# A new order for the 1,035 steps of a sparse-attention and SwiGLU kernel on one core

## The chip, the cores and the metric

The kernel runs on one core of one Trainium2 chip. The metric is the device time of one execution in microseconds (us). The time before is the median of three runs, 237.2 us (235.59, 237.2 and 237.91). A profile of one execution gives the start and the duration of each instruction on each engine: TensorE (PE), its weight loads (PEld), VectorE (DVE), ScalarE (ACT), GpSimd (POOL) and SyncE (SP), which here does nothing but start transfers.

## The reference

Two things are computed, one after the other. First, attention with four batches, eight heads, 768 positions and head size 64, in which each query sees the first 8 keys ("global") and the last 96 before it ("local"), with a bias that falls linearly with distance:

```python
scores = q @ k.T / sqrt(64)
keep   = (key < 8) | ((query - key >= 0) & (query - key < 96))
dist   = where(global and not local, 96, abs(query - key))
scores = where(keep, scores - slope[head] * dist, -1e9)   # slope = 2 ** -(head + 1)
a      = softmax(scores)
attn   = a @ v                                             # 4 x 8 x 768 x 64
```

Then the heads of each position are laid side by side, and the 3,072 rows of 512 pass a gated feed-forward layer:

```python
x    = attn as (3072, 512)
g    = x @ w_gate            # 512 -> 1536
out  = (g * sigmoid(g) * (x @ w_val)) @ w_out   # 1536 -> 512
```

Inputs and outputs are fp32; the kernel computes with fp16 operands and sums in fp32.

## The kernel before

**One list sets the order.** The kernel is written as some forty small functions, each of which issues one step: one load, one group of matmuls, one exponential, one copy. A string, `ORDER` (from line 67), names 1,035 steps with their arguments, such as `g.2.6` or `Lr.3.0.4`. A table (L757) maps each name to its function, and one loop runs the list from the front to the back:

```python
for step in ORDER.split():
    name, *args = step.split(".")
    WORK[name](*(int(a) if a.isdigit() else a for a in args))
```

Scheduling is manual (`tc.manual_schedule()`), so each engine runs its own instructions in the order in which they stand in this list, and nothing is moved between them. The waits between engines follow from the data: a step waits for what it reads, and for the last user of a buffer that it takes. What is planned here is nothing but the position of each step among those of its engine, and, for steps with a letter at their end, the engine: V is VectorE, A is ScalarE, P is GpSimd, and S is a transfer started by SyncE.

**Attention.** Batch 0 comes in two halves of 384 positions, since TensorE has nothing else to do at the start. Its first two head pairs are loaded as fp32 (`Lf`, started by SP and ScalarE) and cast to fp16 (`cast`); all else is loaded by GpSimd, whose transfers cast on the way: key and query halves (`Lh`), four heads of batch 1 (`L4`, L333), single heads of batches 2 and 3 (`Lr`, L344; the arguments are batch, 0 for keys or 1 for queries, and head), value chunks (`Lv`, L292; batch and one of seven chunks), gate and value weights (`Lw`, L351) and output weights (`Lo`, L356). Keys and queries are turned by TensorE (`T`, `U`) with a copy out of PSUM (`k`, `q`, `kw`, `qw`), or by a transposing transfer that SP starts (`D`, L483) into `kN` or `qT`; `K` (L490 to L493) spreads transposed keys into chunks of 120 behind the 8 global ones.

Scores (`C` early, `c` later, L520) go to PSUM, ScalarE takes exponentials of them into `at` (`E`, `x`, L530), VectorE multiplies by masks (`m`, L539), which ScalarE has made from distances (`M`, L384). TensorE then sums the probabilities (`w`, L597 and L630) and weighs the values (`V` for the first half of batch 0; `W`, L614). VectorE inverts the sums (`i`), `j` copies them beside each other, `r` spreads them, and `p` scales the weighed values into `xT`, the input of the feed-forward layer.

Each batch has a value buffer `vS`. Its unused rows are cleared (`Z`, L307 to L310, two memsets). The eight global rows, which arrive with chunk 0, are copied into the later chunks (`G`, L296 to L305): by a transfer of SP, or by an engine. `X` (L319) copies the values to the other half of the partitions.

**Feed-forward.** The 3,072 tokens are eight tiles of 384. For each tile t and each of twelve blocks f of 128 columns there are a gate product (`g.t.f`) and a value product (`v.t.f`), four matmuls of 128x384 each (L693), then a tanh on ScalarE (`t`), and two operations on VectorE (`s` and `h`), which fill `hT`. Output products (`o`, L734, three matmuls of 512 columns each, four steps for each 128 tokens) and the store (`e`) follow. Tiles 0 and 1 are batch 0, and so on; feed-forward work of one batch stands among the attention of the next.

**Buffers.** PSUM is eight banks. A step takes one or two of those that are free at its place in the list, in a fixed rule, and `release` gives them back; so the list also decides which bank a step gets, and for whose last reader it waits. Buffers in SBUF rotate: a new tile of a tag takes the buffer that has been out longest. The tags `kst` and `qst` (staging of keys and queries) have two buffers, `vS` two, `vX` two, `kN` two, `qT` four, `xT` four, `hT` three. A staging tile comes into being with the first load that asks for its batch:

```python
def stage(b, i):
    if (b, i) not in stages:
        shape = [128, H, J * D] if b == 1 else [128, NP, J, 2, D]
        stages[b, i] = sb2.tile(shape, FP16, name=("kst", "qst")[i], tag=("kst", "qst")[i])
    return stages[b, i]
```

In the order before, the keys' staging is asked for by batch 0 (fp32 and fp16 tiles), then batch 1, 2 and 3, and `vS` by batch 0, 1, 3 and 2 (`Z.3.P` stands ahead of `Z.2.P`).

Of the kernel before, what the change touches and what calls it, by code (L numbers as in the profile page):

```python
# [73 lines left out]
E.2.1 r.0.0.0.0 G.0.1.4.V Lw.0.2.1 E.3.1 r.0.0.0.1 b.2.0 E.3.0 T.0.1.0 C.2.0 q.3.1.V k.0.1.A E.2.0  # L74
T.3.1.0 T.0.1.1 T.2.1.0 T.1.1.0 T.1.1.1 k.1.1.A k.3.1.V q.0.1.A q.1.1.V w.0.0.1 Lw.1.0.0 k.2.1.V
q.2.1.A c.0.0.1.1 i.0.0.1 V.1 V.2 V.0 Lw.0.2.0 r.0.1.0.1 Lv.0.5 B.1.1.1 M.0.1 p.0.0.0.0.V Lv.0.6
p.0.0.0.1.V x.0.0.1.1 c.0.1.1.1 B.1.1.0 r.0.1.0.0 Lv.0.4 x.0.1.1.1 p.0.1.0.0.V V.3 c.0.0.1.0 Ld.P.0
c.0.1.1.0 p.0.1.0.1.V X.0.0.2.4.V Lw.1.2.1 Lw.1.2.0 L4.0.0 M.1.1 Lr.1.0.5 Lr.1.0.7 x.0.0.1.0 g.0.0
g.0.3 g.0.1 g.0.2 x.0.1.1.0 m.0.0.1.1.V L4.1.0 t.0.3 t.0.0 m.0.0.1.0.V Lr.1.0.6 w.0.1 v.0.3 t.0.2
s.0.3 v.0.2 s.0.0 i.0.1 s.0.2 Lr.1.1.6 t.0.1 Lw.0.1.1 v.0.0 h.0.2 j.0.1.A X.0.1.2.4.A Lr.1.0.4 h.0.0  # L80
Lr.1.1.4 Lw.0.1.0 g.0.8 g.0.9 r.0.0.1.1 t.0.8 D.1.3.0 X.0.0.4.7.A s.0.1 s.0.8 r.0.0.1.0 r.0.1.1.0
g.0.10 Lw.1.1.0 Lr.1.1.7 h.0.3 v.0.1 Lr.1.1.5 X.0.1.4.7.A t.0.10 t.0.9 h.0.1 s.0.10 g.0.11 W.0.1.0
W.0.1.1 v.0.8 p.0.0.1.1.V p.0.0.1.0.V v.0.10 v.0.9 D.1.2.0 D.1.3.1 r.0.1.1.1 p.0.1.1.0.V v.0.11
p.0.1.1.1.V g.1.10 v.1.3 s.0.9 t.0.11 t.1.10 g.1.0 s.0.11 h.0.10 g.1.1 U.1.0 h.0.8 h.0.11 h.0.9
Z.3.P s.1.10 U.0.1 U.1.1 U.0.0 t.1.0 s.1.0 t.1.1 g.1.11 kw.1.V kw.0.A v.1.10 v.1.1 qw.0.A Lv.1.6
qw.1.A g.1.2 g.1.8 g.1.3 t.1.11 s.1.1 s.1.11 t.1.8 v.1.0 t.1.3 t.1.2 h.1.10 h.1.1 M.1.0 s.1.3 v.1.2
g.0.6 h.1.0 v.1.11 s.1.8 g.1.9 s.1.2 Lv.1.1 M.0.0 g.1.6 h.1.2 Lw.1.1.1 h.1.3 t.1.9 g.0.5 s.1.9
Lr.2.1.3 h.1.11 c.1.0.0.0 t.0.6 t.0.5 t.1.6 s.0.6 c.1.0.0.1 x.1.0.0.1 D.1.2.1 v.1.8 Lv.1.5 g.1.4
s.1.6 g.0.7 g.0.4 h.1.8 s.0.5 v.1.9 v.0.6 Lr.2.0.4 Lv.1.0 t.0.7 x.1.0.0.0 s.0.7 M.3.0 h.1.9 K.1.3
Lo.0 Lo.1 g.1.7 t.0.4 v.1.6 c.1.0.1.0 h.0.6 t.1.7 s.0.4 s.1.7 v.0.7 Lo.2 Lr.2.0.0 h.1.6 v.1.4 Lv.1.2  # L90
h.0.7 v.1.7 t.1.4 g.1.5 v.0.4 Lv.1.4 s.1.4 v.0.5 Lv.1.3 h.1.7 t.1.5 v.1.5 K.1.2 h.1.4 h.0.4 Lr.2.0.3
h.0.5 c.1.1.1.1 Lr.2.1.2 c.1.1.0.0 x.1.0.1.0 c.1.1.0.1 s.1.5 h.1.5 M.2.1 o.0.1.0 o.0.2.0 x.1.1.1.1
# [717 lines left out]
```

## Time and profile before

| | |
|---|---|
| median of three runs | 237.2 us (235.59 to 237.91) |
| span of the profiled execution | 235.1 us, which is also the only time that the profile gives for it |
| instructions | 6,093 |
| TensorE clock granted | 1.000 of full speed |
| data moved by transfers | 25.97 MB, most of it in GpSimd's queue |
| TensorE busy | 228.1 us, 97% of the span |
| VectorE, ScalarE, GpSimd busy | 166.8, 117.0 and 79.1 us |

The profile's first block gives the busy time of each engine and its share of the span. A row of the chain of waits has a start, a duration, and the line that held the end up at that time. A row of the instruction groups names the engine, line and operation, the tile written and the tile read, and a count; behind it stand the total busy time and the mean of one in ns. A row of the timeline has a start, a duration, an engine and a line; in square brackets stands how long the engine was idle ahead of it, and what ended that. In a row of the waits, the operation that waited stands to the left of the arrow and what it waited for to the right, then the idle time in us, the count, and the longest one. A row of the stretches has start and end, length, and then, for TensorE, its weight loads, VectorE, ScalarE and GpSimd, the busy time and the number of instructions; the last columns are the granted clock, the DMA share and the GB/s.

### The profile page before, as it was taken

What the parts mean: (1) busy time and instruction counts of PE and PEld (TensorE: products, weight loads), DVE (VectorE), ACT (ScalarE), POOL (GpSimd) and SP (SyncE); (2) the same over time, 40 slices, a digit from 0 to 9 for tenths busy, and PEclk for the clock granted to TensorE, in tenths of its full rate; (3) what the DMA queues carried; (4) which work ended last, traced back from release to release, by engine and by line L of the source; (5) the groups of instructions that cost most, each with busy time, mean ns of one, the idle gap of its engine ahead of it and who ended that gap; (6) DMA issues with size and microseconds to landing.
All of it is one profiled execution on the core that took longest, in us unless ns stands there. A gap on an engine that the chain in (4) does not pass through costs nothing.

```text
span 235.1 us, 6093 instructions
## 1 busy us (share of the span) xinstructions
PE 228.1 (97%) x2504; PEld 132.2 (56%) x2504; DVE 166.8 (71%) x385; ACT 117.0 (50%) x220; POOL 79.1 (34%) x113
## 2 busy tenths in 40 slices
PE   7889999998899999999999999999999999999997
PEld 5556556555455656655555565556655565554444
DVE  2698996888549798877798998979776467461020
ACT  4679736783546703827826687744231334140421
POOL 8985778664264079787700000000000000000000
DMA  6999999999999999999999610200000120000323
GB/s 170 190 179 205 203 189 185 130 137 146 202 149 163 204 163 136 110 144 138 146 179 197 68 47 3 89 3 0 3 0 0 45 92 1 0 25 22 134 91 134
DMA packets 88324, 25.97 MB, mean 110 GB/s; under 512 B 78048, under 2 KB 85256, under 8 KB 88296
## 3 DMA queue, kind: packets, MB, share of 16 engines
q0 software_dynamic: 67120, 14.25, 78.7%
q1 hardware_dynamic: 20488, 10.74, 24.5%
q10 hardware_dynamic: 688, 0.59, 0.7%
q8 instruction: 19, 0.31, 0.6%
q14 instruction: 9, 0.07, 0.1%
HBM read 28.93 MB, written 6.29 MB: 150 GB/s over the span
## 4 chain that ended last, share of the span: by engine, by line
PE 65%; DMA 23%; POOL 6%; DVE 3%; issue 1%; ACT 0%; SPq 0%; DVEq 0%; POOLq 0%; ACTq 0%
PE banks L693 39%; PE banks L734 20%; DMA vS<-in_v_dram 6%; DMA kst<-in_k_dram 5%; DMA wv<-in_moe_w_val_dram 4%; DMA qst<-in_q_dram 4%; DMA k<-in_k_dram 3%; PE banks L614 2%; PE banks L520 2%; POOL vS L292 1%; DMA out_dram<-osb 1%; PE banks L723 1%; POOL qst L344 1%; POOL q L284 1%; PE banks L630 1%
## 5 line engine op out<-in xcount | busy, mean ns | idle before, releaser
L699 ACT ACTIVATE th<-banks 128x384 f32<-128x384 f32 x96 | 43.9, 493 | 68.1 <-PE banks L693 66.5
L693 PE MATMUL banks<-xT,wv 128*128 128x384 f16 x384 | 71.7, 326 | 0.4 <-DMA wv<-in_moe_w_val_dram 0.3
L693 PE MATMUL banks<-xT,wg 128*128 128x384 f16 x384 | 70.6, 326 | 0.0
L709 DVE TENSOR_TENSOR hT<-banks,sl 128x384 f16<-128x384 f32 x96 | 50.9, 551 | 22.8 <-PE banks L693 19.8
L734 PE MATMUL banks<-wo,hT 128*128 128x512 f16 x276 | 65.3, 379 | 0.6 <-DMA wo<-in_moe_w_out_dram 0.6
L703 DVE SCALAR_TENSOR_TENSOR sl<-th,banks 128x384 f32<-128x384 f32 x96 | 50.2, 546 | 19.3 <-ACT th L699 18.8
L693 PEld LDWEIGHTS <-wv 128*128 128x128 f16 x384 | 36.8, 98 | 26.3 <-DMA wv<-in_moe_w_val_dram 0.7
L693 PEld LDWEIGHTS <-wg 128*128 128x128 f16 x384 | 37.2, 98 | 25.5 <-DVE xT L678 0.2
L734 PEld LDWEIGHTS <-hT 128*128 128x128 f16 x276 | 26.3, 98 | 29.2 <-DMA wo<-in_moe_w_out_dram 0.8
L530 ACT ACTIVATE at<-banks 128x1008 f16<-128x1008 f32 (+3 forms) x28 | 25.7, 957 | 10.6 <-PE banks L520 9.6
L292 POOL DMA_DIRECT2D vS<-in_v_dram x28 | 25.1, 906 | 5.9 <-DMA qst<-in_q_dram 3.0
L752 ACT ACTIVATE osb<-banks 128x512 f32<-128x512 f32 x23 | 13.5, 597 | 20.0 <-PE banks L734 16.5
L539 DVE TENSOR_TENSOR at<-at,masks 128x1008 f16<-128x1008 f16 (+3 forms) x26 | 16.2, 645 | 5.3 <-ACT at L530 4.9
L344 POOL DMA_DIRECT2D qst<-in_q_dram x20 | 16.8, 843 | 8.4 <-DMA wo<-in_moe_w_out_dram 5.2
L344 POOL DMA_DIRECT2D kst<-in_k_dram x20 | 16.7, 839 | 5.5 <-DMA wo<-in_moe_w_out_dram 2.0
L663 DVE STREAM_TRANSPOSE rb<-dR 128x384 f32<-128x384 f32 x32 | 17.1, 555 | 0.1
L678 DVE TENSOR_TENSOR xT<-banks,rb 128x384 f16<-128x384 f32 x22 | 11.0, 542 | 1.0 <-PE banks L614 0.8
L319 ACT COPY vX<-vS 64x1792 f16<-64x1792 f16 (+2 forms) x7 | 9.0, 1287 | 3.3 <-DMA vS<-in_v_dram 3.1
L520 PEld LDWEIGHTS <-kT 64*64 64x64 f16 x456 | 7.4, 107 | 5.5 <-issue 5.1
L520 PE MATMUL banks<-qT,kT 64*64 64x152 f16 (+9 forms) x456 | 9.1, 214 | 0.9 <-DMA qT<-qst 0.7
L614 PE MATMUL banks<-at,vS 64*64 64x152 f16 (+9 forms) x228 | 8.0, 213 | 0.4 <-DVE hT L709 0.4
L614 PEld LDWEIGHTS <-vS 64*64 64x64 f16 x228 | 6.7, 107 | 2.4 <-issue 2.4
(77 smaller groups left out, 150.6 us busy)
## 6 DMA issues: line engine op xcount, KB each, us to landing
out_dram<-osb SPq DMA_DIRECT2D x23, 256.0 KB, 2.5
vS<-in_v_dram POOLq DMA_DIRECT2D x24, 120.0 KB, 8.4
kst<-in_k_dram POOLq DMA_DIRECT2D x20, 96.0 KB, 7.5
qst<-in_q_dram POOLq DMA_DIRECT2D x20, 96.0 KB, 7.2
wg<-in_moe_w_gate_dram POOLq DMA_DIRECT2D x6, 256.0 KB, 8.1
wv<-in_moe_w_val_dram POOLq DMA_DIRECT2D x6, 256.0 KB, 8.4
wo<-in_moe_w_out_dram POOLq DMA_DIRECT2D x3, 512.0 KB, 13.5
k<-in_k_dram POOLq DMA_DIRECT2D x3, 192.0 KB, 6.0
```

The source lines that it names most:

```text
L292: nc.gpsimd.dma_start(out=v_of(b)[r0:r0 + n, c, heads(g), :], in_=v[b, heads(g), KC * c:KC * c + n, :].rearrange("h p d -> p h d"))
L344: nc.gpsimd.dma_start(out=rows_of(i, b, h // 2)[:, :, h % 2, :], in_=KQ[i][b, h].rearrange("(t p) d -> p t d", p=128))
L520: nc.tensor.matmul(sc[64 * r:64 * r + 64, hi, col:col + n], lhsT=kTs[2 * g + r][d, k0:k0 + 64], rhs=qTs[b, 2 * g + r][d, q0:q0 + n], start ...
L530: nc.scalar.activation(out=at[:, :, 0:w], in_=sc[:, :, 0:w], func=AF.Exp, scale=scale)
L539: ENG[e].tensor_mul(a2, a2, masks[:, 2 * g:2 * g + 2, x:x + w])
L614: nc.tensor.matmul(num[64 * hi:64 * hi + 64, r, q0 - HB * half:q0 - HB * half + n], lhsT=vSs[b][k, c, h] if up == r else crossed[b][k, c, ...
L663: nc.vector.transpose(rb.rearrange("p (n i) -> p n i", i=32), rbs[b, half][:, g, r].unsqueeze(2).broadcast_to([128, TB // 32, 32]))
L693: nc.tensor.matmul(gv[t, f, which][:, 0:TB], lhsT=w[:, c, 128 * f:128 * f + 128], rhs=xTs[t][:, c, :], start=(c == 0), stop=(c == NC - 1))
L699: nc.scalar.activation(out=th, in_=gv[t, f, 0][:, 0:TB], func=AF.Tanh, scale=0.5)
L703: nc.vector.scalar_tensor_tensor(out=sl, in0=gv[t, f, "t"], scalar=1.0, in1=gv[t, f, 0][:, 0:TB], op0=AluOp.add, op1=AluOp.mult)
L709: nc.vector.tensor_mul(hTs[t][:, f, :], gv[t, f, 1][:, 0:TB], gv[t, f, "s"])
L734: nc.tensor.matmul(ops_t[t, i], lhsT=hTs[t][:, f, 128 * i:128 * i + 128], rhs=wo[:, f, :], start=(f == 0), stop=(f == NFF - 1))
```

## The change

The string `ORDER` is replaced by another; no function is touched. It holds the same 1,035 steps. 24 of them have another engine letter, all others differ in their place alone. The changes that matter for the steps of the prediction:

- **Start.** `kz` and one clear (`Z.0.P`) lead GpSimd's work; the second clear (`Z.1`) goes to VectorE, further back. The early table `Ld.S.2` is SP's first load. `fill.10` stands ahead of `fill.5`. Three casts move to ScalarE and one to VectorE; key copies `k.1.0` and query copy `q.3.0` go to VectorE, `k.3.1`, `q.2.0` and `q.3.1` to ScalarE, `q.2.1` to VectorE. Keys and queries of both halves of batch 0 (`Lh`) are loaded ahead of all but one value chunk; then three chunks come in a row (`Lv.0.2 Lv.0.1 Lv.0.3`) and two gate weights in a row (`Lw.0.0.0 Lw.0.0.1`). The global rows `G.0.4.7` go from SP to VectorE.
- **Sums of the second half** (`w.0.1`): the gate products `g.0.0` and `g.0.1` no longer stand ahead of it, and mask `M.1.1` is made earlier, `M.3.1` later.
- **Loads of the middle.** Batch 1's loads are ordered anew. `Lr.3.0.4` now stands ahead of `Lr.2.0.7`: batch 3's keys ask for staging before batch 2's. The three output weights follow `Lr.2.0.7` at once, and six of the seven value chunks of batch 1 follow these.
- **Clears and copies later.** `Z.2` and `Z.3` go from GpSimd to VectorE, and batch 2's clear stands ahead of batch 3's. `G.2.1.7` goes from SP to VectorE. Some of `j` and `X` and three of `kw` and `qw` change between VectorE and ScalarE.
- All feed-forward steps stand in another order too, down to the last output products.

```diff
 ORDER = """
-pre Z.0.P Lf.A.1.1 Lf.S.0.1 fill.5 Z.1.P Lf.A.1.0 kz.P Li cast.0.1.V cast.1.0.V cast.1.1.A fill.10
-sl.1 Lh.0.0.4.8 sl.2 Ld.P.1 sl.0 T.1.0.0 T.1.0.1 Ld.S.2 sl.3 T.0.0.1 k.1.0.A sl.4 q.1.0.A q.0.0.V
-b.1.1 Lf.S.0.0 Lh.1.0.4.8 sl.5 sl.7 cast.0.0.V b.1.0 Lh.1.1.4.8 C.1.1 Lv.0.0 C.1.0 E.1.1 Lh.0.1.0.4
-T.0.0.0 b.2.1 b.0.0 E.1.0 k.0.0.V sl.6 b.0.1 T.2.0.0 T.3.0.0 C.0.1 k.2.0.V k.3.0.V Lh.1.1.0.4
-Lh.0.1.4.8 C.0.0 Lv.0.3 Lv.0.1 T.3.0.1 Lv.0.2 E.0.1 T.2.0.1 E.0.0 q.2.0.V G.0.4.7.S pk b.3.0
-Lw.0.0.0 Lw.0.0.1 q.3.0.A w.0.0.0 b.3.1 i.0.0.0 Lw.1.0.1 T.3.1.1 M.3.1 C.3.0 T.2.1.1 C.2.1 C.3.1
...
-g.0.3 g.0.1 g.0.2 x.0.1.1.0 m.0.0.1.1.V L4.1.0 t.0.3 t.0.0 m.0.0.1.0.V Lr.1.0.6 w.0.1 v.0.3 t.0.2
...
-Z.3.P s.1.10 U.0.1 U.1.1 U.0.0 t.1.0 s.1.0 t.1.1 g.1.11 kw.1.V kw.0.A v.1.10 v.1.1 qw.0.A Lv.1.6
...
-s.1.6 g.0.7 g.0.4 h.1.8 s.0.5 v.1.9 v.0.6 Lr.2.0.4 Lv.1.0 t.0.7 x.1.0.0.0 s.0.7 M.3.0 h.1.9 K.1.3
-Lo.0 Lo.1 g.1.7 t.0.4 v.1.6 c.1.0.1.0 h.0.6 t.1.7 s.0.4 s.1.7 v.0.7 Lo.2 Lr.2.0.0 h.1.6 v.1.4 Lv.1.2
...
-W.1.1.0 h.2.6 W.1.1.1 Z.2.P v.2.3 Lr.3.1.7 s.2.0 p.1.1.1.1.V e.0.1 p.1.1.1.0.V g.2.9 r.1.0.1.1
...
-c.2.1.0.0 c.2.1.0.1 x.2.1.0.1 o.2.2.1 o.2.2.2 t.3.7 G.2.1.7.S K.2.0 Lv.2.5 o.2.2.3 Lr.3.1.1 v.3.11
...
+Ld.S.2 Li Lf.A.1.0 pk pre kz.P Lf.S.0.1 sl.2 Lf.S.0.0 Z.0.P fill.10 Lh.0.0.4.8 Lf.A.1.1 sl.3 sl.7
+sl.0 fill.5 cast.1.0.A Lh.1.0.4.8 cast.1.1.V cast.0.1.A b.1.0 cast.0.0.A sl.6 T.0.0.1 T.1.0.0 sl.1
+sl.5 Ld.P.1 T.1.0.1 b.1.1 q.1.0.A T.0.0.0 Lh.0.1.4.8 q.0.0.V T.2.0.0 k.1.0.V Lv.0.0 b.0.1 k.0.0.V
+C.1.0 C.1.1 T.3.0.1 k.2.0.V q.3.0.V T.3.0.0 E.1.0 C.0.1 Lh.1.1.4.8 E.1.1 sl.4 Lh.0.1.0.4 b.0.0 C.0.0
+T.2.0.1 E.0.1 E.0.0 Lh.1.1.0.4 k.3.0.V Lv.0.2 b.3.0 Lv.0.1 b.3.1 b.2.1 Lv.0.3 w.0.0.0 q.2.0.A
+Lw.0.0.0 Lw.0.0.1 Z.1.V Lw.1.0.1 M.1.1 C.3.1 G.0.1.4.V C.2.1 Lw.1.0.0 E.2.1 i.0.0.0 E.3.1 C.3.0
+G.0.4.7.V T.3.1.1 T.3.1.0 T.2.1.1 b.2.0 Lw.0.2.0 E.3.0 k.3.1.A C.2.0 E.2.0 q.2.1.V T.0.1.0 T.1.1.1
...
+p.0.1.0.1.V g.0.3 g.0.2 x.0.1.1.0 x.0.1.1.1 Lw.1.2.0 t.0.2 m.0.0.1.1.V m.0.0.1.0.V Lw.1.2.1 w.0.1
...
+D.1.3.0 h.1.10 s.1.3 Lr.3.0.4 h.1.2 D.1.3.1 Lr.2.0.7 Lo.0 g.0.6 t.1.8 t.0.6 v.1.9 v.1.8 s.1.8
+D.1.2.1 Lo.1 h.1.3 v.1.1 t.1.9 s.1.9 M.3.0 h.1.8 g.1.5 h.1.1 g.1.6 s.0.6 t.1.5 g.1.7 g.0.4 h.1.9
+t.1.6 Lo.2 s.1.5 c.1.0.0.1 c.1.0.0.0 v.1.6 s.1.6 t.1.7 M.2.1 x.1.0.0.0 g.0.7 Lv.1.4 Lv.1.2 v.1.5
+h.1.6 x.1.0.0.1 v.0.6 Z.2.V s.1.7 g.0.5 K.1.3 v.1.7 K.1.2 g.1.4 v.0.7 t.0.7 Lv.1.5 t.0.5 M.0.0 s.0.7
+Lv.1.6 Lv.1.1 h.1.5 v.1.4 h.0.6 v.0.4 s.0.5 t.1.4 v.0.5 t.0.4 h.1.7 s.1.4 Lv.1.3 s.0.4 Lr.2.0.5
...
+D.2.0.0 g.3.11 Lv.3.0 t.2.5 h.3.1 Lv.3.4 s.2.5 c.2.1.1.1 t.3.2 s.3.2 x.2.1.1.1 D.2.1.1 v.2.8 s.2.10
...
+c.2.0.0.1 s.3.6 c.2.0.0.0 x.2.0.0.0 o.2.1.1 g.3.7 v.3.0 o.1.1.0 m.2.0.1.1.V o.2.1.2 G.2.1.7.V
...
 """
```

More of the change, by code (lines that the diff above doesn't have):

```diff
@@ new lines @@
+W.2.1.1 p.2.0.0.1.V r.2.1.1.1 o.2.0.2 r.2.1.0.1 p.2.1.0.0.V o.2.0.3 n.2.1.1 v.3.3 p.2.1.0.1.V g.4.11
+r.2.1.1.0 g.4.3 g.4.1 h.3.10 e.2.0 K.3.3 g.4.8 D.3.1.0 t.4.11 t.4.3 h.3.3 v.4.11 Lv.3.6 s.4.3 s.4.11
+h.4.11 v.4.1 t.4.8 s.4.8 t.4.1 g.4.6 K.3.0 v.4.8 s.4.1 t.4.6 c.3.1.1.1 x.3.1.1.1 p.2.1.1.1.V
+c.3.1.0.0 x.3.1.0.0 s.4.6 g.4.10 p.2.1.1.0.V h.4.8 o.3.1.0 o.3.1.1 K.3.1 c.3.1.0.1 h.4.1 r.2.0.1.0
+t.4.10 Lv.3.1 Lr.3.1.2 c.3.1.1.0 D.3.1.1 x.3.1.0.1 v.4.3 o.3.1.2 o.3.1.3 v.4.2 x.3.1.1.0 m.3.1.0.0.V
@@ L147 @@
+o.7.1.3 o.7.0.0 e.7.1 o.7.0.1 o.7.0.2 o.7.2.0 o.7.0.3 o.7.2.1 o.7.2.2 e.7.0 o.7.2.3 e.7.2 fill.7
+fill.4 e.7.3 fill.2
 """
```

124 lines of the change are left out of this document (57 added, 67 removed).

## The prediction

> **What bounds the kernel now.** I read the page's busy table first, then four stretches of the span, then what TensorE waited for, and last the chain that ended last.
>
> ```profile
> span 235.1 us, 6093 instructions
> PE 228.1 (97%) x2504; PEld 132.2 (56%) x2504; DVE 166.8 (71%) x385; ACT 117.0 (50%) x220; POOL 79.1 (34%) x113
> ```
>
> TensorE is busy for 228.1 of 235.1 us. The same span, cut where its work changes character (columns: stretch, its length, then busy time of each engine):
>
> ```profile
> 0.00:21.12 21.12, 17.87 (x307) 11.66 (x308) 14.66 (x52) 14.23 (x27) 18.37 (x37) 1.00 1.35 184
> 21.12:71.36 50.24, 48.48 (x598) 28.30 (x587) 38.93 (x85) 30.93 (x53) 31.23 (x40) 1.00 1.78 168
> 71.36:152.00 80.64, 80.25 (x1144) 46.99 (x1143) 70.14 (x162) 47.20 (x92) 29.55 (x37) 1.00 1.47 126
> 152.00:235.10 83.10, 81.46 (x477) 45.30 (x469) 43.11 (x87) 24.69 (x51) 0.00 (x0) 1.00 0.12 42
> ```
>
> The first stretch ends with the first feed-forward product, the second with the weighing of batch 1's values, the third with the last score work. TensorE is idle for 3.25 us (21.12 less 17.87), 1.76, 0.39 and 1.64 us. The first includes the start, the last the tail; only about 2 us in the middle are stalls that an order could remove or enlarge. These are they:
>
> ```profile
> PE banks L520 <- DMA qT<-qst: 0.7, 1, 0.7
> PE banks L734 <- DMA wo<-in_moe_w_out_dram: 0.6, 1, 0.6
> ...
> PE banks L614 <- DVE hT L709: 0.4, 1, 0.4
> ```
>
> Two of the three are transfers, transposed queries (0.7) and output weights (0.6). The chain tells why (start, duration, what):
>
> ```profile
> 15.14 9.38 DMA wv<-in_moe_w_val_dram
> ...
> 43.39 10.97 DMA kst<-in_k_dram
> ...
> 54.65 14.83 DMA vS<-in_v_dram
> ...
> 82.78 0.67 PE banks L614 x30
> ...
> 152.08 20.91 PE banks L693 x128
> ...
> 224.24 3.88 PE banks L734 x18
> ```
>
> Until about 83 us the end is set by loads that GpSimd issues one behind another; each takes 9 to 15 us to land, because many are in flight. From there TensorE runs without a break: 128 products in 20.91 us are 163 ns each, so a step of four costs 0.65, and 18 output products in 3.88 us make a step of three 0.65. The change neither adds nor removes a product, so this floor stays. What can move is the distance by which TensorE lags behind its own work when it comes out of the loads, and any stall made after that.
>
> I add up step costs in both orders (0.65 for each product or output step, fills and scores by their rows in the trace). That work ahead of a step, against the time at which the step ran, gives the lag. It is a count of steps, and I use it for differences only.
>
> **The change, part by part.** First the start.
>
> ```profile
> 0.73 1.41 POOL L309 MEMSET vS<- 32x256 uint32 x4 [0.29 <-POOLq L791]
> ...
> 21.29 1.85 ACT L530 ACTIVATE at<-banks 128x976 f16<-128x976 f32 x2
> ...
> 23.83 0.64 PE L630 MATMUL banks<-at,pick 128*32 128x128 f16 x36
> ```
>
> GpSimd clears two value buffers ahead of its first load, four memsets in 1.41 us; in the new order it clears one, so the first load leaves 0.7 us earlier. Two casts more and one early key copy less on ScalarE lie beside the fills and the first landings. The second clear now stands on VectorE behind key copies; I cost it between nothing and 0.7 (GpSimd's price for two memsets) and take nothing, as VectorE waits there for the first V chunk anyway. Keys and queries of both halves lead V: the first eleven loads are the same eleven, so the last of the first four V chunks lands at the same place in the queue, up to 0.7 earlier. The sums of the second half's probabilities (L630, 23.83) waited for four exponentials on ScalarE, the last of which ended at 23.14 (21.29 and 1.85). In the new order the step has two products fewer ahead of it, 14.8 us of work in place of 16.1, and so would come 1.3 us sooner; but ScalarE still owes the four exponentials.
>
> ```profile
> L384 ACT ACTIVATE masks<-dist 128x992 f16<-128x992 f16 (+1 forms) x8 | 7.8, 989 | 0.0
> L305 DVE COPY vS<-vS 8x1536 f16<-8x1536 f16 x1 | 0.9, 898 | 0.0
> ```
>
> One mask (0.99) is moved behind them, and a key copy of about half that ahead of them. ScalarE then ends at 22.2 to 23.1, and the step starts at 22.4 to 23.3. The lag becomes 7.6 to 8.5, where it was 7.7. The global rows of V for chunks 4 to 6 also leave SP for VectorE: 0.90 (L305), ahead of the first half's scaling. That removes most of VectorE's lead, which is why I don't count the 0.7 as won. Sum for the start: 0, with −0.1 and +0.8 as ends; below that the earlier load could win 0.6.
>
> Second, the loads of 30 to 70 us, where I expect the decision.
>
> ```profile
> 37.16 3.75 SPq L483 DMA_TRANSPOSE kN<-kst  x2
> ...
> 48.34 2.25 POOL L356 DMA_DIRECT2D wo<-in_moe_w_out_dram  x3 [1.43 <-DMA qst<-in_q_dram]
> ...
> 58.26 0.82 PE L520 MATMUL banks<-qT,kT 64*64 64x160 f16 x44 [0.68 <-DMA qT<-qst]
> 59.71 4.13 PE L734 MATMUL banks<-wo,hT 128*128 128x512 f16 x18 [0.64 <-DMA wo<-in_moe_w_out_dram]
> ```
>
> I count kilobytes in GpSimd's queue, as the page lists them per load, and divide by the 168 GB/s of the second stretch. Batch 1's last value chunk is behind 9,588 KB before and 9,492 KB after: 0.6 us sooner. The first output weights move from 8,108 to 7,820 KB: 1.7 sooner. Both keep their place only if the queue never stops, and there I see a new stop. Key staging has two buffers, dealt in the order in which batches first ask. The new order asks for batch 3 (one row load) before batch 2, so batch 2 gets batch 1's buffer, and its first load must wait until the last transposing DMA of batch 1's keys has read it. Queued behind that load are the three output weights and six of batch 1's seven value chunks.
>
> When does that transpose land? It ran at 37.16 behind 5,492 KB; after, its row is behind 6,412 KB, 5.5 us later, less 0.7: 42.0. SP also holds the broadcast of batch 1's global rows ahead of it, which waits for a value chunk behind 6,220 KB, and the other key transpose; with their issues (the two at L483 span 3.75) I take 43.5.
>
> ```profile
> kN<-kst SPq DMA_TRANSPOSE x1, 8.3
> wo<-in_moe_w_out_dram POOLq DMA_DIRECT2D x1, 512.0 KB, 11.3
> qst<-in_q_dram POOLq DMA_DIRECT2D x1, 96.0 KB, 4.1
> ```
>
> With the 8.3 us that it took among loads, it lands at 51.8. GpSimd resumes, and issues the first output weights at 53.0; before it was 48.34. Their landing took 11.3 us behind seven other loads; the queue is now nearly drained, and the nearest row is the load that started on an idle queue, 4.1 us for 96 KB; the other 416 KB at 168 GB/s are 2.5 more. So they land at 59.6, and before at 59.7 (48.34 and 11.3). The last value chunk follows 1,672 KB later, 10.0 us: 69.6, and before 69.48 (54.65 and 14.83). I take 0 for this stretch. Ends: −1.3, if the transpose lands early and the stop is empty (0.6 and 0.7), and +1.6, if the queries' last transpose, whose rows are 376 KB further back, holds up the scores by 2.2 less 0.7.
>
> Third, what VectorE takes over later. Clears of batches 2 and 3 leave GpSimd:
>
> ```profile
> 83.66 0.68 POOL L309 MEMSET vS<- 32x256 uint32 x2 [10.61 <-issue]
> ```
>
> This clear held GpSimd for 10.61 us, because batch 2 had the buffer that batch 1 was still using. That stop goes; another replaces it, since the first chunk of batch 3 now waits for VectorE's clear, which stands at about 95 us. As 22 loads are left there, against 32 at 83.66, I cost it at nothing: rows for batch 3's scores were needed 40 us later. If GpSimd's cover is gone, each microsecond there costs one.
>
> Batch 2's global rows go from SP to VectorE as one copy of twice L305's width, by that row 1.8 us, just where eight mask products and four other steps queue for the sums of batch 2. Two PSUM banks that those sums need are freed behind it. Walking VectorE's order by the spacing of its rows, the second sum comes 0.85 us late. Against it, the 0.4 us wait on hT (L614) has more room in the new order. Sum: +0.45. The upper end adds two more places where VectorE's order is tight, batch 1's sums ahead of its last scaling (0.45) and batch 3's masks (0.4): +1.7 in all; the lower end is −0.4, if the 1.8 us find slack.
>
> All together 0 + 0 + 0.45: the span goes from 235.1 to about 235.5. The profiled execution is given by its span; the three timed runs lie 0.5 to 2.8 us above it, their median 2.1. With that median's 2.1 I get 237.6.
>
> **The rivals.** *A later stop (slower).* The stop at batch 2's first key load decides from the point at which the transpose lands after about 52. If the weights, issued at 53.0, take the full 11.3, they land at 64.3, 4.7 later than before. TensorE has steps that don't need them for less than 1 us there, so some 3.7 are lost: 241.3. For it speaks that both stalls of today sit at this place (58.26 and 59.71); against it that the queue drains meanwhile, so nothing competes.
>
> *An empty stop (faster).*
>
> ```profile
> DMA to landing us min/median/max: 3.4/5.9/8.6
> L492 DVE COPY kT<-kN x10: 158/172/637, 51.5 to 133.1; 128x48 f16<-128x48 f16 x10
> ```
>
> If the transpose takes 3.4, it lands at 46.9, before GpSimd would have come to the load. Then queue and start win 1.3 together, the waits of 0.7 and 0.6 shrink with it, the 0.4 on hT goes and VectorE's copy is hidden. With the 0.6 of a start that does win, 2.3 to 2.9: 235.0 at the most cautious, 234.7 by the middle. Against it: the small transposes ran among no loads, these do.
>
> *VectorE's copies stretched while GpSimd writes descriptors (slower).* One copy of 128x48 took 637 ns at most, 172 in the median. Three clears of two memsets and two copies of global rows newly run on VectorE while GpSimd issues loads; eight times 0.465 is 3.7 if each lies on the path: 241.3. [...] The median shows that it seldom decides here.
>
> *The order changes nothing* is part of the forecast: each engine's program order differs, but a step whose inputs come late starts late in either order.
>
> **How the numbers follow.** About 1% either way is what a measurement of this kernel can tell from no change: below 234.8 faster, above 239.6 slower. Forecast 0.53; the later stop 0.21; stretched copies 0.05; the empty stop 0.18, its middle just inside faster; 0.03 for mishaps. Faster 0.19, same 0.54, slower 0.27: small parts of the forecast's own range, −1.8 to +4.1 from its ends (−0.1 and −1.3 and −0.4; 0.8 and 1.6 and 1.7), lie over both limits. All ends meeting is unlikely, so the range runs from 234.8, the empty stop, to 241.0, most of the later stop.
>
> **What would show it.** Start: the sums at L630 begin near 22.5 rather than 23.83, behind two products. Loads: wo issued by GpSimd near 53, with an idle time ahead that a transpose (kN) ended; if GpSimd shows no such idle time, the buffers are not dealt as I read them and the second part is wrong. The weights land near 59.6; the weighing at L614 begins near 71. Later: a copy at L305 of about 1.8 us near 110, and a wait of the sums (L630) near 114; no wait there means that the third term is nothing. A TensorE idle time of several us between 50 and 70 would make the prediction wrong to the slow side, and fewer than 1 us in all after 25 us to the fast side.

## The result and the profile after

The new order takes 239.73 us in the median of four executions (239.05 to 240.01). The old order, timed beside it, takes 236.39. The ratio is 1.0127, with a 95% interval of 1.0092 to 1.0162. A ratio, here and below, is to the old order timed beside the kernel, and leaves out the disturbed executions. The new order is slower by a little over 1%, 2.1 us above the forecast of 237.6, on the slow side of it and inside its range. Timed a second time, unchanged (as `a_again` below), it took 238.75 beside 236.35, a ratio of 1.0105 (1.0068 to 1.0141). The span of a profiled execution lies 1.8 us below its time here (240.01 and 238.2).

The page of the new order gives its span and its busy engines:

```profile
span 238.2 us, 6096 instructions
PE 230.1 (97%) x2504; PEld 133.3 (56%) x2504; DVE 172.0 (72%) x404; ACT 113.6 (48%) x209; POOL 78.8 (33%) x107
PEclk9799999999999999999999999999999999999999
```

TensorE is busy 2.0 us longer (230.1 against 228.1) and idle 1.1 longer (8.1 against 7.0), with the same 2,504 products. A part of the longer busy time goes with the third line: the granted clock falls to 0.7 in the second of forty slices, where the old order's page shows no such line. The same stretches as in the prediction, and what is left behind them:

```profile
0.00:21.12 21.12, 17.20 (x273) 11.47 (x274) 13.45 (x49) 13.20 (x28) 17.60 (x35) 0.92 1.33 182
21.12:71.36 50.24, 49.49 (x580) 28.89 (x580) 40.83 (x91) 32.23 (x58) 32.51 (x41) 1.00 1.70 176
71.36:152.00 80.64, 79.94 (x1151) 46.49 (x1149) 71.22 (x169) 43.90 (x75) 28.69 (x33) 1.00 1.13 120
152.00:235.10 83.10, 82.54 (x510) 45.87 (x498) 46.45 (x97) 24.30 (x51) 0.00 (x0) 1.00 0.10 38
```

In the first 21 us TensorE gets through 273 products where the old order did 307, and the clock is 0.92. Between 21 and 71 us it idles 0.75 (50.24 less 49.49) where it idled 1.76: in this execution the stalls of the middle are gone. What it waits for now:

```profile
PE banks L417 <- ACT k L400: 1.9, 2, 1.4
PE banks L394 <- DVE ones L362: 1.5, 1, 1.5
PE banks L693 <- DVE xT L678: 0.6, 1, 0.6
PE banks L693 <- DVE hT L709: 0.6, 1, 0.6
```

The three rows that the prediction began with (transposed queries 0.7, output weights 0.6, hT at L614 0.4) don't appear. In their place TensorE waits for casts of keys at the start (1.9) and twice for VectorE ahead of a feed-forward product (0.6 each). So this profile offers two suspects: the start, and VectorE. The experiments had to say which of them makes the time.

### The profile page after: what moved, and what is told of

The parts are those of the page before. It is cut to its first block, busy times and chain, and to the rows that moved or that the text cites. A ratio compares the mean times of both kernels' runs of the same rounds, so it can differ in the third digit from the quotient of the medians.

```text
span 238.2 us, 6096 instructions
## 1 busy us (share of the span) xinstructions
PE 230.1 (97%) x2504; PEld 133.3 (56%) x2504; DVE 172.0 (72%) x404; ACT 113.6 (48%) x209; POOL 78.8 (33%) x107
## 4 chain that ended last, share of the span: by engine, by line
PE 67%; DMA 12%; DVE 11%; ACT 3%; POOL 2%; issue 2%; SPq 1%; DVEq 0%; POOLq 0%
PE banks L693 41%; PE banks L734 18%; DMA wo<-in_moe_w_out_dram 4%; DMA k<-in_k_dram 2%; DMA qst<-in_q_dram 2%; DVE xT L678 2%; DMA kN<-kst 2%; DVE at L539 2%; PE banks L520 2%; DVE rb L663 2%; PE banks L614 1%; DVE sl L703 1%; POOL kst L344 1%; PE banks L723 1%; DVE dT L647 1%
## 5 line engine op out<-in xcount | busy, mean ns | idle before, releaser
L693 PE MATMUL banks<-xT,wg 128*128 128x384 f16 x384 | 72.1, 326 | 1.7 <-DVE xT L678 0.6
L693 PE MATMUL banks<-xT,wv 128*128 128x384 f16 x384 | 72.6, 326 | 0.2
L709 DVE TENSOR_TENSOR hT<-banks,sl 128x384 f16<-128x384 f32 x96 | 50.9, 549 | 23.9 <-PE banks L693 23.3
L734 PE MATMUL banks<-wo,hT 128*128 128x512 f16 x276 | 67.2, 379 | 0.1
L292 POOL DMA_DIRECT2D vS<-in_v_dram x28 | 25.7, 931 | 20.1 <-PE banks L693 17.2
L344 POOL DMA_DIRECT2D qst<-in_q_dram x20 | 17.5, 887 | 2.4 <-DMA wo<-in_moe_w_out_dram 2.0
L539 DVE TENSOR_TENSOR at<-at,masks 128x1008 f16<-128x1008 f16 (+3 forms) x26 | 15.7, 637 | 2.3 <-ACT at L530 2.2
L678 DVE TENSOR_TENSOR xT<-banks,rb 128x384 f16<-128x384 f32 x22 | 11.3, 545 | 1.7 <-issue 1.5
L647 DVE STREAM_TRANSPOSE dT<-banks 128x384 f32<-128x384 f32 x9 | 5.1, 572 | 4.9 <-PE banks L630 3.9
L384 ACT ACTIVATE masks<-dist 128x992 f16<-128x992 f16 (+1 forms) x8 | 7.9, 1006 | 0.0
L614 PE MATMUL banks<-at,vS 64*64 64x152 f16 (+9 forms) x228 | 7.8, 213 | 0.0
```

The source lines that it names most:

```text
L292: nc.gpsimd.dma_start(out=v_of(b)[r0:r0 + n, c, heads(g), :], in_=v[b, heads(g), KC * c:KC * c + n, :].rearrange("h p d -> p h d"))
L344: nc.gpsimd.dma_start(out=rows_of(i, b, h // 2)[:, :, h % 2, :], in_=KQ[i][b, h].rearrange("(t p) d -> p t d", p=128))
L539: ENG[e].tensor_mul(a2, a2, masks[:, 2 * g:2 * g + 2, x:x + w])
L678: ENG[e].tensor_mul(x, nums[b, g, half][:, r, 0:TB], rb)
L693: nc.tensor.matmul(gv[t, f, which][:, 0:TB], lhsT=w[:, c, 128 * f:128 * f + 128], rhs=xTs[t][:, c, :], start=(c == 0), stop=(c == NC - 1))
L709: nc.vector.tensor_mul(hTs[t][:, f, :], gv[t, f, 1][:, 0:TB], gv[t, f, "s"])
```

## The experiments

**The start first, since the profile shows most there.** SP now issues the early table and the identity ahead of the first keys. The old order's timeline has the first load on SP and the cast of these keys (L400) like this:

```profile
0.74 0.45 SPq L280 DMA_DIRECT2D k<-in_k_dram  x1
...
3.89 0.36 DVE L400 CAST k<-k 128x384 f16<-128x384 f32 x1 [2.48 <-DMA k<-in_k_dram]
```

and the new order:

```profile
1.60 1.03 SPq L280 DMA_DIRECT2D k<-in_k_dram  x2
...
6.54 0.51 ACT L400 CAST k<-k 128x384 f16<-128x384 f32 x1 [2.36 <-DMA k<-in_k_dram]
```

The load leaves 0.86 us later, and its cast starts 2.65 later. Two experiments separate the load from the engine of the cast. The first moves one step:

```diff
-Ld.S.2 Li Lf.A.1.0 pk pre kz.P Lf.S.0.1 sl.2
+Lf.S.0.1 Ld.S.2 Li Lf.A.1.0 pk pre kz.P sl.2
```

> The new order with one step moved: the first key load (Lf.S.0.1) is again the first that SP issues, ahead of the early table and the identity. Theory A (the start: SP issues the first keys 0.86 us later, TensorE waits for their cast, and its clock is halved for 3.4 us): the first key cast on ScalarE starts near 4.2 us in place of 6.54, the granted clock stays at 1.00 in the first 25 us, the sums at L630 start near 22.2 in place of 24.28, and as the output weights have 5 us of room, the whole gain of 2.1 is kept: about 237.6, against 239.7. Theory B (the casts on ScalarE are what is late): about 239.7, because the casts stay on ScalarE. Theory C (GpSimd's first load, 0.6 us earlier, takes the bandwidth from the keys): the cast starts near 5.5, half of the gain, 238.7.

Measured: 238.61 us, ratio 1.0077 (1.0043 to 1.011). The wait for the keys went, and another took its place: the bias step that stands ahead of the transposes now waited for the scaled identity, which had become SP's third load.

```profile
6.25 0.90 PE L554 MATMUL banks<-early,slopeI 128*128 128x432 f16 x2 [1.41 <-DVE slopeI L379]
```

The second puts the four casts back on their old engines:

```diff
-cast.1.0.A ... cast.1.1.V cast.0.1.A ... cast.0.0.A
+cast.1.0.V ... cast.1.1.A cast.0.1.V ... cast.0.0.V
```

> The new order with the four casts on the engines of the old one (three on VectorE, cast.1.1 on ScalarE), all in the new places. Theory A (the keys land late, whoever casts them): 239.7, the key casts still start near 6.5 and 7.9 us and the granted clock still drops near 8.6. At the most 0.3 less, as VectorE casts in 0.36 where ScalarE takes 0.51. Theory B (ScalarE's casts are the late part): TensorE's 1.4 us of waiting ahead of T.1.0.0 goes, about 237.8.

Measured: 238.49 us, ratio 1.0095 (1.0056 to 1.0133). TensorE still waited until 7.18 us for the first key transposes, as it had until 7.11. The casts' engine is not the cause. This profile beside the new order's also shows what the clock column can miss. The same two products of 432 columns in three timelines: in the old order,

```profile
10.42 0.54 PE L554 MATMUL banks<-early,slopeI 128*128 128x432 f16 x2
```

in the new order,

```profile
11.32 0.87 PE L554 MATMUL banks<-early,slopeI 128*128 128x432 f16 x2
```

and with the casts moved.

```profile
11.57 0.90 PE L554 MATMUL banks<-early,slopeI 128*128 128x432 f16 x2
```

The stretch around them, in the new order,

```profile
10.00:12.00 2.00, 2.00 (x26) 1.03 (x20) 1.42 (x8) 1.62 (x3) 1.99 (x3) 0.50 1.83 179
```

and with the casts moved (the clock is the third column from the end):

```profile
10.00:12.00 2.00, 2.00 (x26) 1.19 (x22) 1.95 (x10) 1.55 (x3) 1.94 (x3) 1.00 1.65 176
```

The products take 0.54, 0.87 and 0.90, so TensorE ran far below its full rate in both later cases; the clock column says 0.50 in one and 1.00 in the other.

Third, idle products on TensorE (fills) where it waits for the casts, on the guess that they keep its rate up without a load or a cast being moved:

```diff
-T.0.0.1 T.1.0.0 sl.1 sl.5 Ld.P.1 T.1.0.1 b.1.1 q.1.0.A T.0.0.0
+T.0.0.1 fill.12 T.1.0.0 sl.1 sl.5 Ld.P.1 T.1.0.1 b.1.1 q.1.0.A fill.4 T.0.0.0
```

> The new order with 16 more idle products on TensorE: 12 ahead of T.1.0.0 and 4 ahead of T.0.0.0, where TensorE waits for the keys' casts (1.4 and 0.5 us). The casts stay where they are. This tells the clock from the waiting. If the half clock itself costs time: the granted clock stays at 1.00, T.1.0.0 still starts near 7.1, and the steps from there to 12 us take 1.2 to 1.6 us less, about 238.3. If the engines behind TensorE set the pace there and the clock is only a mark of the waiting: 239.7, or up to 0.3 more.

Measured: 239.3 us, ratio 1.0099 (1.0054 to 1.0144). In its profile the clock column gives 1.00 in every stretch of 2 us up to 18 us (0.65 and 0.50 from 8 to 12 us in the first profile of the new order), and the first feed-forward products come 1.0 us sooner than in the first profile of the new order. Yet the time is that of the new order (239.73 and 238.75). The fills didn't buy what the profile seemed to promise.

**The new order itself, again.** No change to the kernel.

> The new order itself once more, unchanged, beside the kernels of this call. If the wait for the keys' casts and the half rate behind it come in every execution, 239.7 again (239.2 to 240.1) and TensorE is about 2 us late at the first feed-forward product. If the landing of the first keys changes from execution to execution, as one earlier run with the same start shows, which was 2 us earlier there, the median comes out lower, near 238.5, with a spread of 2 us.

Measured: 238.75 us, and its profiled execution has a span of 236.4. In this execution the keys' cast starts at 5.44 and the sums at L630, which started at 24.28 in the first profile, come two microseconds sooner; the two products of 432 columns take 0.53 again. Its timeline, and then what its TensorE waited for:

```profile
9.76 0.53 PE L554 MATMUL banks<-early,slopeI 128*128 128x432 f16 x2
...
22.37 0.64 PE L630 MATMUL banks<-at,pick 128*32 128x128 f16 x36
```

```profile
PE banks L417 <- ACT k L400: 1.0, 2, 0.7
PE banks L693 <- DVE xT L678: 0.8, 1, 0.8
PE banks L693 <- DVE hT L709: 0.6, 1, 0.6
```

So the two lost microseconds of the start belong to some executions and not to others of the same kernel; the two waits for VectorE are in both, the first of them a little longer here. Counted as the lag behind the step work, this execution is about level with the old order's profile at the first feed-forward tile (0.1 us behind).

**The two waits for VectorE.** The old order's profile has the small copies of line L659 on ScalarE alone (count, then the least, median and greatest time in ns, and the first and last start in us):

```profile
L659 ACT COPY dR<-dR x28: 206/208/211, 25.5 to 148.7; 32x24 f32<-32x24 f32 x28
```

VectorE's timeline around the two waits, in the new order:

```profile
75.89 1.27 DVE L659 COPY dR<-dR 32x24 f32<-32x24 f32 x4
77.20 1.02 DVE L678 TENSOR_TENSOR xT<-banks,rb 128x384 f16<-128x384 f32 x2
...
152.01 0.72 DVE L659 COPY dR<-dR 32x24 f32<-32x24 f32 x4
```

The first four copies (`j.1.1`) stand ahead of the last two scalings (L678) of tile 2, and TensorE's products of that tile wait for these. They are of use only to the spreads of the other half, which come later. The same four copies of batch 3 (`j.3.1`) stand ahead of the hidden product at 155.29 that frees a bank for the next product. The experiment gives both back to ScalarE:

```diff
-j.1.1.V ... j.3.1.V
+j.1.1.A ... j.3.1.A
```

> The new order with j.1.1 and j.3.1, four small copies each, back on ScalarE. Theory A (they stand on VectorE's path to the last scaling of a tile, 1.27 us near 76 and 0.72 near 152): TensorE's stalls ahead of g.2.2 (1.02 us) and g.4.7 (0.72 us) shrink to under 0.3 each; 239.7 less 1.3 to 1.7, about 238.2. If something else holds these products, or ScalarE comes to the copies just as late, 239.4 to 239.8.

Measured: 236.53 us, ratio 0.9998 (0.9968 to 1.0029). That is 2.2 us less than the new order's second median and 3.2 less than its first (2.5 and 3.0 by the ratios, since the three were not timed together), more than the 1.3 to 1.7 expected; the loss is gone. The scalings now start as soon as the reciprocals are done, and VectorE waits for ScalarE's copies behind them, where nobody needs it; no wait for L678 or L709 is left in TensorE's list. VectorE's timeline with the copies on ScalarE:

```profile
73.89 0.95 DVE L678 TENSOR_TENSOR xT<-banks,rb 128x384 f16<-128x384 f32 x2
76.16 1.04 DVE L663 STREAM_TRANSPOSE rb<-dR 128x384 f32<-128x384 f32 x2 [1.31 <-ACT dR L659]
```

On TensorE this kernel runs the same products in the same order as the new one, so the two profiled executions can be set side by side, product by product. The first products of tile 2 in the second profile of the new order:

```profile
74.89 0.33 PE L693 MATMUL banks<-xT,wg 128*128 128x384 f16 x1
76.03 1.60 PE L693 MATMUL banks<-xT,wg 128*128 128x384 f16 x7 [0.81 <-DVE xT L678]
```

and with the copies on ScalarE, where the eight run without a break:

```profile
75.03 1.46 PE L693 MATMUL banks<-xT,wg 128*128 128x384 f16 x8
```

Ahead of this place the new order is 0.15 us early, behind it 1.13 late, which is 1.28 lost; at 154 us it loses another 0.72, and nowhere else between 60 us and TensorE's last product more than 0.02. So 2.0 of the 2.2 us between the two spans (236.4 and 234.2) are lost at these two places. The remainder is 0.4 behind TensorE's last product, less the 0.15.

One of the two alone:

```diff
-j.1.1.V
+j.1.1.A
```

> The new order with only j.1.1 back on ScalarE, j.3.1 stays on VectorE. If the two stalls add up, each at its own price: the first (1.0 to 1.3 us ahead of g.2.2) goes, the second (0.72 ahead of g.4.7) stays: 237.3 to 237.8, a ratio of 1.004 to 1.005. If a microsecond won near 76 us is lost again later: a ratio of 1.009 or more.

Measured: 236.77 us, ratio 1.0018 (0.9992 to 1.0044). The stall ahead of the first products of tile 2 is gone, that at 152 us is still in its list (L709, 0.6), and TensorE falls back by 0.73 there against the profile with both on ScalarE. So most of the loss comes from the first four copies (1.0105 to 1.0018). What the second four cost in the median, 0.2% or 0.5 us, is too small to be told from their 0.72 or from nothing: the intervals overlap.

Is it the engine, or the place on the engine? Both copies stay on VectorE, behind the work that doesn't need them:

```diff
-j.1.1.V e.1.2 p.1.0.0.1.V o.0.1.3 p.1.1.0.0.V Lr.3.1.3
+e.1.2 p.1.0.0.1.V o.0.1.3 p.1.1.0.0.V j.1.1.V Lr.3.1.3
-j.3.1.V v.5.4 ... p.3.1.0.1.V h.5.4
+v.5.4 ... p.3.1.0.1.V h.5.4 j.3.1.V
```

> The new order with the copies j.1.1 and j.3.1 left on VectorE but moved back in its order: j.1.1 behind the scaling p.1.1.0.0, j.3.1 behind the hidden product h.5.4. If the place is what costs (nothing in those scalings and that product needs the copies, they only queue behind them): the stalls ahead of g.2.2 and g.4.7 go as they went with the copies on ScalarE, 236.3 to 236.9, a ratio to the old order of 1.000. If VectorE has too much work there whatever its order: the stalls move to the next products, 238.0 or more, a ratio above 1.006.

Measured: 237.07 us, ratio 1.0029 (1.0007 to 1.0052), between the two cases and near the first. The place accounts for about three quarters of the loss (1.0105 to 1.0029); a rest of 0.3% stays. The profile shows one new wait of 0.4 us for L678, near 153: where `j.3.1` now stands, another scaling queues behind it, and TensorE falls back by 0.54 there against the profile with the copies on ScalarE.

And the copies on VectorE in the old order, in their old places:

```diff
-j.1.1.A ... j.3.1.A
+j.1.1.V ... j.3.1.V
```

> The old order with one thing of the new: the copies j.1.1 and j.3.1 on VectorE in place of ScalarE, in the old places. If these copies are what delays the last scaling of a tile wherever they stand: 0.7 to 1.3 us each in VectorE's order, a stall ahead of the first products of tiles 2 and 6, 1.2 to 1.7 us slower than the old order (about 238.1). If VectorE has room there in the old order and only the new neighbours (a transpose and two reciprocals right ahead of the copies) leave none: within 0.4 of the old order.

Measured: 237.17 us, ratio 1.0027 (0.9992 to 1.0061): not to be told from the old order. Its profile has no wait for L678 or L709 at tiles 2 and 6. (It does show the old stalls of the middle grown to 1.5 for transposed queries and 1.4 for output weights, so that these also differ between executions.) The same two letters that cost 1% in the new order cost at most 0.6% here, the upper end of the interval, and perhaps nothing. More than the neighbours differs, though. In this profile GpSimd stands still while the first four copies run, and they take 0.72 us, not 1.27 or 1.52 as in the new order's two profiles. VectorE's timeline, and then GpSimd's, whose idle time ahead of this row begins near 75:

```profile
76.41 0.72 DVE L659 COPY dR<-dR 32x24 f32<-32x24 f32 x4
...
85.22 0.67 POOL L309 MEMSET vS<- 32x256 uint32 x2 [10.18 <-DMA qT<-qst]
```

And the profiled execution, the slowest of the ten, starts the weighing of batch 1 some 1.9 us later than the old order's profile does, which gives VectorE time. The run doesn't show which of these spares the old order.

**The stop of GpSimd.** The prediction's second part turned on this. It is there, in the new order's timeline:

```profile
48.37 0.82 POOL L344 DMA_DIRECT2D kst<-in_k_dram  x1 [7.20 <-DMA kN<-kst]
```

and in its chain of waits:

```profile
43.18 4.54 DMA kN<-kst
...
50.65 10.39 DMA wo<-in_moe_w_out_dram
```

GpSimd stands still for 7.2 us, and the last output weights land at 61.04 (50.65 and 10.39). Without the stop, on top of the copies on ScalarE:

```diff
-D.1.3.0 h.1.10 s.1.3 Lr.3.0.4 h.1.2 D.1.3.1 Lr.2.0.7 Lo.0
+D.1.3.0 h.1.10 s.1.3 h.1.2 D.1.3.1 Lr.2.0.7 Lo.0
...
-Lr.3.0.7
+Lr.3.0.4 Lr.3.0.7
```

> The new order with both copies on ScalarE, and batch 3's first key row (Lr.3.0.4) moved back to just ahead of Lr.3.0.7, so that batch 2's keys get the free staging buffer. GpSimd no longer stops for 7 us behind Lr.3.0.4: the output weights are issued near 42 us in place of 49. If the stop costs nothing (the weights have 3 us of room and land sooner on a drained queue): the same as with the stop, a ratio of 0.998 to 1.003. If the stop holds something up, up to 1 us faster, 0.996 or less; if the drained queue helps the middle, up to 1 us slower, 1.004 or more.

Measured: 240.67 us, ratio 1.0171 (1.013 to 1.0212). That is 4.1 us slower than with the stop (236.53), four times the largest effect that I had allowed for. Its timeline, and what its TensorE waited for:

```profile
41.29 2.25 POOL L356 DMA_DIRECT2D wo<-in_moe_w_out_dram  x3
...
57.61 0.35 DVE L490 COPY kT<-kN 128x720 f16<-128x720 f16 x1 [4.63 <-DMA kN<-kst]
```

```profile
PE banks L693 <- DVE sl L703: 3.5, 1, 3.5
```

The output weights now leave at 41.29, together with the transposing DMAs of batch 1's keys. With 1.5 MB of weights and the value chunks behind them in flight, the transposed keys reach VectorE at 57.6, where in the new order's first profile they had landed at 47.72 (43.18 and 4.54); they were issued at the same time in both, the second near 43. VectorE waits 4.63 us for them, and TensorE 3.5 for the products queued behind that on VectorE. The wait has a second price. Behind it TensorE runs at half rate for a while, and falls back by another 1.3 us against the profile with the stop. The stretch behind the wait has a clock of 0.50:

```profile
62.00:64.00 2.00, 2.00 (x54) 1.33 (x53) 2.00 (x6) 0.74 (x1) 1.43 (x2) 0.50 3.31 137
```

The stop is no cost: with it the two transposes landed 5.2 and 4.5 us after their issue, and without it, with the loads that it holds back in flight, they took up to 14.6.

**The old start, the new rest.** The first 70 steps of the old list (up to `w.0.0.0`), in its order and on its engines, then the rest of the new; once as it is, and once with the copies on ScalarE.

```diff
-Ld.S.2 Li Lf.A.1.0 pk pre kz.P Lf.S.0.1 ...
+pre Z.0.P Lf.A.1.1 Lf.S.0.1 fill.5 Z.1.P ... q.3.0.A w.0.0.0
 b.3.1 Lw.1.0.1 M.1.1 C.3.1 ...
```

> The new order with the whole start of the old one: the old list's steps up to w.0.0.0, in its order and on its engines, then all other steps as in the new order. If the start costs what the two profiles differ by there: the lag at the first feed-forward products falls by 2.1 us, the stalls ahead of g.2.2 and g.4.7 stay at 1.0 and 0.7, and the time is 1 to 2 us below the new order's in this call. If a later wait (the output weights, the loads of 60 to 70 us) takes the place of the start, the time stays within 0.4 of the new order's.

> The old start, the rest of the new order, and j.1.1 and j.3.1 on ScalarE. If the new order's middle gains what its profile shows (the old stalls of 0.7 on transposed queries, 0.6 on output weights and 0.4 on hT are gone there), this is faster than both: 0.8 to 1.4 us below the old order, about 235.4. If the gain of the middle only existed because TensorE came late from the start, the stalls come back and the time is the old order's, 236.3 to 237.0.

Measured: 241.3 us, ratio 1.0175 (1.0115 to 1.0236; three of the four executions within 241.24 to 241.52, one at 238.27), and, with the copies on ScalarE, a ratio of 1.0055 (1.0015 to 1.0095), with executions that spread over more than 3 us from 236.02 upwards. Both starts were worse than either of the two that they were put together from. The old start issues the keys of heads 4 to 7 of the second half as GpSimd's eighth load, where the new one has them fourth, and the new order's TensorE turns them sooner than the old one did; in the first of the two it waited 3.0 us for them, by its list of waits:

```profile
PE banks L417 <- DMA k<-in_k_dram: 3.0, 1, 3.0
```

The wait isn't in every execution: the profiled one of the second kernel, its fastest, waits only 0.2 for these keys. So these two say nothing on the gain of the middle, for which they were made. They do give the copies' price a second time, roughly, since the wait spreads both: 1.0175 less 1.0055 is 1.2%.

**A start with the keys first that avoids the wait of the first experiment**, with both copies on ScalarE:

```diff
-Ld.S.2 Li Lf.A.1.0 pk pre kz.P Lf.S.0.1 ... b.1.0 cast.0.0.A sl.6 T.0.0.1 T.1.0.0 sl.1 sl.5 Ld.P.1 T.1.0.1
+Lf.S.0.1 Ld.S.2 Li Lf.A.1.0 pk pre kz.P ... cast.0.0.A sl.6 T.0.0.1 T.1.0.0 sl.1 sl.5 Ld.P.1 T.1.0.1 b.1.0
```

> The new order with both copies on ScalarE, the first key load first on SP, and the bias step b.1.0, which waits for the early table, moved behind the first key transposes, so that TensorE meets the keys first. If the late first keys and the half rate behind them are what spreads the new order's start: T.1.0.0 starts near 4.9 in place of 5.8 to 7.1, the matmuls run at full rate from there in most executions, and the time is 235.6 to 236.3, below the old order, with fewer slow executions. If the start is bound by the casts or by the later loads of the second half: as with the copies alone, a ratio of 0.999 to 1.001.

Measured: 236.35 us, ratio 0.9991 (0.9964 to 1.0018): no faster than the copies on ScalarE alone, with a narrower spread (235.88 to 237.21, where those had 235.15 to 237.97). The keys' cast ended at 5.24, but TensorE then waited 0.7 us for the identity, and the half rate was not avoided in this execution: two products of 432 columns took 0.90 at 7.13. No version here beats the old order by more than the measurement can tell.

## Why the prediction was right or wrong

**The number.** The time lies inside the range of 234.8 to 241.0, and that is owed more to the width of the range than to the sum. As a change, the forecast was +0.4 us (237.2 to 237.6), and the two measurements are +3.3 and +2.4. The old order's own time, 236.4 beside the new one, lies 0.8 below the 237.2 that I started from, and this hides a part of the miss. By my own limit of 239.6 the first measurement is just on the slower side, which had 0.27.

**The first term, the start (0, with −0.1 and +0.8), held in one execution and not in the other.** The sums at L630 were forecast for 22.4 to 23.3, behind two products: 22.37 in the second profile, 24.28 in the first. The step that was missing is SP's: I counted GpSimd's first load as 0.7 us earlier and did not count that the same edit puts two tables ahead of the first keys on SP. In the two profiled executions their cast came 1.6 and 2.7 us later than in the old order (5.44 and 6.54, against 3.89). And I took TensorE's rate as given. When it waited there, it then ran at half rate for some 3.4 us in the first of them (a mean clock of 0.65 from 8 to 10 us and 0.50 from 10 to 12). Nonetheless the start isn't what makes the loss: moving the keys' load or the casts, or filling the wait, changed the ratio from 1.0127 and 1.0105 to between 1.0077 and 1.0099, with intervals that overlap, and keys first with late bias changed 0.9998 to 0.9991. I had made the start my leading theory after the first profile; it fell. Whether it accounts for the 1.0 us between the two medians of the same kernel (239.73 and 238.75) no run shows.

**The second term, the loads of 30 to 70 us (0, with −1.3 and +1.6), was right in its mechanism, and took the stop for a cost or for nothing where it is a gain.** The buffers were dealt as I read them, and GpSimd's stop is ended by a transpose (kN). The transpose was forecast to be issued at 43.5 and was issued at 43.18; I gave it 8.3 us and it took 4.54, nearer to the 3.4 of the rival "an empty stop". The stop itself was not empty: GpSimd stood for 7.2 us, where that rival has the transpose land before GpSimd comes to the load. The weights were forecast to be issued at 53.0 and were issued from 49.2 on (48.37 and 0.82); the first of them took 6.4 us to land, where I had 6.6 on a drained queue. Counted as lag, TensorE gains 1.1 us there between the old profile and the second profile of the new order, near the end of −1.3. What I had not seen is the other direction: I asked what the stop holds up, and not what the loads behind it would do to the transposes. The run without the stop answers: it is 4.1 us slower in the median.

**The third term, VectorE (+0.45), is the step that failed: the cost was put on the wrong operation.** I put the cost on the copy of batch 2's global rows: 1.8 us near 110, with a wait of the sums near 114. The copy took half of that, and no such wait is in the list, which by my own sign makes this term nothing. VectorE's timeline in the new order:

```profile
110.36 0.94 DVE L305 COPY vS<-vS 8x3072 f16<-8x3072 f16 x1
```

Twice the columns (8x3072) cost the same 0.9 as the single width (8x1536, 0.898 in the old order), so my scaling by width was wrong. The cost was at the place that I had carried as the upper end, "batch 1's sums ahead of its last scaling (0.45)". There stand a transpose, two reciprocals and now four copies ahead of two scalings. The prediction doesn't price the change of engine of these copies at all, nor those of batch 3. The price of both is 2.2 us by the medians (238.75 less 236.53). The idle times, 0.6 to 0.8 and 0.6, don't add up to that, but the comparison product by product does nearly: 1.28 at the first place, almost three times the 0.45 that I gave it, and 0.72 at the second, which I had at nothing. A stall costs more than its idle time because a product normally starts 0.16 us before the end of the one ahead of it, by the profile's ends (one takes 0.33, eight in a row 1.46), and at a break this overlap is lost too. At the first place there are two breaks, 0.81 and 0.14, and with twice 0.16 they make the 1.28; at the second, 0.55 and 0.16 make the 0.72. Open is only why 0.4 more lies behind TensorE's last product.

**The rivals.** The later stop didn't come: the transpose landed at 47.7, well ahead of 52. The stretched copies had 0.05 and a price that was made of eight of them. In the chain of the second profile they are there, two of them, at the decisive place:

```profile
73.87 0.59 DVE dR L659
...
74.47 0.17 DVE dR L659
...
74.65 0.17 DVE dR L659
...
74.83 0.55 DVE dR L659
```

Two copies of 32x24 take 0.17 and two 0.55 to 0.59, while GpSimd issues loads one behind another; at 152 us in the first profile, with GpSimd done, four take 0.72 in all. So 0.8 of the 1.5 us at this place is stretch. The run with the copies on VectorE in the old order takes GpSimd's loads away from them, since GpSimd stands still there, and all four take 0.17. In each of the new order's two profiles two of the four take longer (0.26 and 0.63 in the first, 0.59 and 0.55 in the second), and these are the ones that run while GpSimd passes from one load to the next; the other two fall inside the issue of one load and take 0.17. The copy of 637 ns in the old order's profile ran over such a passage too (86.23 to 86.87, the next load from 86.83). What this rival's name calls the writing of descriptors is in the traces the issue of a load by GpSimd, 0.69 to 0.97 us each at this place. Why a copy is stretched at such a passage no trace shows. One slip in the rival of the empty stop: 237.6 less 2.3 is 235.3, not 235.0; nothing hangs on it.

**The sum.** By the lag, the second profile of the new order against the old profile is +0.1 (start), −1.1 (middle), +0.7 (first copies), +1.0 (second copies and pieces under 0.15 us), and +0.5 behind TensorE's last product: 1.2 us, where the spans 236.4 and 235.1 give 1.3. The 0.7 is less than the 1.28 at that place because the old order has its own stall in this stretch, the 0.4 at L614. The medians differ by 2.4, since the old order's profiled execution was 0.5 slower than its median and the new one's 0.5 faster than its own. My range rested on this one old profile, and on stalls in its middle which change between executions.

## What to carry to other kernels

Where an order is exchanged as a whole, look first at which operations change their engine, and for each at what is queued behind it there without needing it: two sets of four small copies made the whole net loss, and with them back on their engine everything else that was moved came to nothing in sum (0.9998). What a stall costs is better taken from the starts of the same products in two profiles than from its idle time, which leaves out the overlap that is lost at each break. Of a queue that stops, ask both ways: who waits for it, and who has the bandwidth to itself meanwhile. Of two executions of the same kernel, a difference in the start of 2 us was not the difference in the medians; a suspect that one profile shows should be looked for in a second one before it is believed.

## What the runs showed of the hardware

- The granted clock's column can say 1.00 while TensorE runs far below full rate: two products of 432 columns took 0.90 us in the stretch that it gives as 1.00 (casts moved, 10 to 12 us), 0.87 in the one that it gives as 0.50 (first profile of the new order), and 0.54 and 0.53 in the old order's profile and the new order's second. The spacing of products of one shape was the safer sign.
- Where the fall is recorded, half rate lasted 3.4 us: in the first profile of the new order the clock was 0.65 from 8 to 10 us (1.4 us at half rate) and 0.50 from 10 to 12. It came after TensorE had waited 1.4 and 0.5 us. In the run without the stop half rate lasted as long (0.67 from 60 to 62 us, 0.50 from 62 to 64, 0.98 from 64 to 66), behind a wait of 3.5 us. What sets this length no run shows.
- The transposing DMAs of batch 1's keys landed 5.2 and 4.5 us after their issue while GpSimd stood still (first profile of the new order), and up to 14.6 us after it among 1.5 MB of weights and the value chunks, in the run without the stop. The weights themselves, 512 KB each, took 8.2 to 8.9 us in the median with the stop and 11.9 without.
- Small copies on VectorE (32x24) took 0.17 us alone and inside the issue of one load by GpSimd, and 0.26 to 0.63 where they ran while GpSimd passed from one load to the next (four of the eight near 74 to 77 us in the new order's two profiles). ScalarE's own took 0.21 throughout (206 to 211 ns in the old order's profile), beside such a passage too.
